# Raw queries, a late scaling on GpSimd, and six places for the inputs

## The chip, the cores and the metric

The kernel runs on one core of one Trainium2 chip. The time is device microseconds of one execution. TensorE does the matrix products, VectorE (DVE), ScalarE (ACT) and GpSimd (POOL) the elementwise work, and SyncE (SP) issues the transfers between HBM and SBUF, the on-chip memory. Matmul results land in PSUM, the banks of which VectorE and ScalarE read here.

## The reference

Retention (linear attention with a decay per head) over a sequence of 768 steps, 2 batches, 8 heads of 64, followed by two feed-forward layers on 1536 tokens of 512 features, 2048 hidden:

```
state = gamma * state + k[t] (outer) v[t]
y[t]  = (1/8) * q[t] . state
x = y as [1536, 512]
h = x @ w_in;   x = silu(h) @ w_out
h = x @ w2_in;  x = leaky_relu(h, 0.01) @ w2_out
```

All arrays are float32.

## The kernel before

**Attention stage.** The sequence is cut into chunks of 128 steps: 12 chunks in all, taken in an order that alternates between the two batches (`ORDER`); j counts them from 0 to 11. The inputs of a chunk come as two transfers of 512 KB (queries with keys, values with keys by row) into one of four places (`att_t`, `load_att`, L98 to L104). For each chunk TensorE computes scores (L200, one chunk ahead), the product of masked scores with values (L219), the product of queries with the running state (L228, not in the first chunk of a batch) and the update of the state (L237, not in the last chunk of a batch). VectorE multiplies the scores with the mask (tile `P`, L207) and adds the update to the decayed state (L250). GpSimd multiplies the keys with their decays (L182) and decays the state (L189).

A row of the result also needs a factor that decays with its position in the chunk, the tile `G`. `G` is spread over the partitions by two small matmuls in chunk 0 (L397) and copied by ScalarE (L401). From chunk 5 on GpSimd multiplies the queries with `G` ahead of the scores (`queries`, L176). For chunks 0 to 4 VectorE multiplies the result with `G` (L258) into an SBUF tile.

The feed-forward products work with float32 numbers cut into a rounded high part and the rest: ScalarE copies the result of a chunk with rounding into `xh` (L262), VectorE subtracts that from the result into `xl` (L263). For chunks 5 to 11 both read the result in PSUM, for chunks 0 to 4 the SBUF tile.

**Feed-forward stage.** Tokens stand in three sets of 512 (chunks 0 to 3, 4 to 7, 8 to 11). `up` (L276) is 12 matmuls per set and block of 128 hidden features, `down` (L304) 12 more. Sets 0 and 1 go through `up` together for one block, then one `down` of set 0: 36 matmuls per turn, and each turn needs two new weights. ScalarE activates each `up` result twice (L287 to L290, into `gf` and into the high part), VectorE subtracts (L291).

Weights come as 64-bit floats and are turned into two float32 parts: two ScalarE copies (`words`, L130, L131), four VectorE steps (`conv1`, L136 and L140; `conv2`, L148 and L152), a ScalarE copy (L161) and a VectorE subtraction (L162, `split_w`). The first two weights are converted in pieces beside the chunks (`piece`), the third in the last chunk, and from there a weight is converted five steps ahead of its use.

**What sets the order.** Nothing is rearranged: each engine executes its instructions in the order in which the code issues them, and waits with semaphores for what an instruction needs. The loop over j (L390 to L421) is that order for the attention stage, the loop over `ops` (L427 to L463) for the rest. A transfer also waits for the eighth before it, by the semaphores of the program.

Of the kernel before, what the change touches and what calls it, by code (L numbers as in the profile page):

```python
# [9 lines left out]
F32 = mybir.dt.float32  # L10
FR = mybir.dt.float32r
# [20 lines left out]
LATE = 5  # L32
# [12 lines left out]
def retention_moe_kernel(ctx: ExitStack, tc: tile.TileContext, att, w1, w2, cst, out):  # L45
# [38 lines left out]
    raw = [gs.tile([128, 2, 512], F32, tag=f"r{i}", name="att_t") for i in range(8)]  # L84
    free = [gs.tile([128, 2, 512], FR, name=f"s{i}") for i in range(21)]

    def widen():
        free.extend(gs.tile([128, 2, 512], FR, tag=f"r{i}", name=f"sr{i}") for i in range(8))
# [9 lines left out]
    def att_t(j, i):  # L98

        return raw[j % 4 * 2 + i // 2][:, i % 2]  # L100

    def load_att(j, *halves):
        for i in halves:
            nc.sync.dma_start(out=raw[j % 4 * 2 + i], in_=att[ORDER[j], :, 2 * i:2 * i + 2])  # L104
# [60 lines left out]
    pt, yu = {}, {}  # L165
# [6 lines left out]

    def queries(j):

        if j >= LATE:
            nc.gpsimd.tensor_tensor(out=att_t(j, 0), in0=att_t(j, 0), in1=G, op=ALU.mult)  # L176
# [33 lines left out]
    def values(j):  # L210
# [3 lines left out]
        yu[j] = y, u = [bank(j % 2 * 2 + i) for i in range(2)]  # L214
# [37 lines left out]
    def store_x(j):  # L252
        b, c = divmod(j, CS)
        y = yu[j][0].rearrange("p (a i) -> p a i", a=NP)
        h, l = (x[b][:, :, c * C:c * C + C] for x in (xh, xl))
        if j < LATE:
            yg = gp.tile([128, NP, C], F32, tag="gf", name="yg")
            nc.vector.tensor_tensor(  # L258
                out=yg, in0=y, in1=G.rearrange("p (a i) -> p a i", a=NP), op=ALU.mult
            )  # L260
            y = yg
        nc.scalar.activation(out=h, in_=y, func=AF.Copy)  # L262
        nc.vector.tensor_tensor(out=l, in0=y, in1=h.bitcast(F32), op=ALU.subtract)  # L263
# [86 lines left out]
    with tc.manual_schedule():  # L350
# [24 lines left out]
        load_att(3, 1)  # L375
        for h in range(H):
            m = M[:, h % 2, (h // 2) * C:(h // 2) * C + C]
            if h < H // 2:
                nc.vector.tensor_scalar(
                    out=m, in0=mask, scalar1=MD[:, h:h + 1], scalar2=None, op0=ALU.mult  # L380
                )
            else:
                nc.scalar.activation(out=m, in_=mask, func=AF.Copy, scale=MD[:, h:h + 1])
# [4 lines left out]
        piece = {5: (conv1, 0), 6: (conv2, 0), 7: (split_w, 0),  # L388
                 8: (conv1, 1), 9: (conv2, 1), 10: (split_w, 1)}
        for j in range(NJ):  # L390
            if j + 1 < NJ:
                queries(j + 1)
                scores(j + 1)
            if j == 0:
                gb = bank(2)
                for r in range(2):
                    nc.tensor.matmul(  # L397
                        out=gb[64 * r:64 * r + 64, :], lhsT=one, rhs=g2[:, r, :],
                        start=True, stop=True,
                    )  # L400
                nc.scalar.activation(out=G, in_=gb, func=AF.Copy)  # L401
            keys(j)
            decay(j)
            values(j)
            if j + 4 < NJ:
                load_att(j + 4, 0, 1)
            if j in (1, 3, 5, 7, 10):
                load_w(early[(1, 3, 5, 7, 10).index(j)])
            if j in (8, 11):
                keep_w(early[(8, 11).index(j)])  # L410
            if j in (5, 8, 10, 11):
                words(early[(5, 8, 10, 11).index(j)])
# [4 lines left out]
            store_x(j)  # L417
            state(j)
            if 5 <= j < NJ - 1:
                step, n = piece[j]  # L420
                step(early[n])  # L421
        split_w(early[2])
        load_w(early[5])
        keep_w(early[2])
        widen()

        for i, op in enumerate(ops):  # L427
# [33 lines left out]
            if i == 1:  # L461
                split_w(early[3])
                keep_w(early[3])  # L463
        for m in range(4):
# [50 lines left out]
```

## Time and profile before

| | us |
|---|---|
| median of three runs | 578.56 (578.34 to 579.38) |
| the profiled execution | 579.3, its span 577.5 |
| TensorE busy | 570.0 (99%) |
| VectorE busy | 285.5 (49%) |
| ScalarE busy | 236.3 (41%) |
| GpSimd busy | 25.3 (4%) |

The attention stage ends at 50.69 us with the first feed-forward matmul (L276). GpSimd's work lies in that stage alone. The granted clock of TensorE is 1.00 over the whole span, its upper level of 2.4 GHz. The shares above are averages over both stages; the rows further down show the stages apart. Times of a row are microseconds from the start of the span.

### The profile page before, as it was taken

Reading aid. Unit: us, or ns where it says so; the run is one execution under the profiler, and the core shown is the slowest. Engines: PE = TensorE matmul, PEld = TensorE weight load, DVE = VectorE, ACT = ScalarE, POOL = GpSimd, SP = SyncE. Lnnn points to the kernel's source line nnn. Section 1 sums busy time; section 2 is a strip of 40 time slices with the busy share of each in tenths; the row PEclk is TensorE's granted clock in tenths of the full one; section 3 lists DMA queues with packets and bytes.
Section 4 is the critical chain, followed back from the end, with each engine's and each line's share of the span. In section 5 each row is a group of like instructions: output and inputs, shape, how many; then the busy total and the mean of one; then the engine's idle time right before and its main releaser. Section 6 shows DMA issues by size and latency. Waiting matters only on the chain.

```text
span 577.5 us, 8037 instructions
## 1 busy us (share of the span) xinstructions
PE 570.0 (99%) x3030; PEld 470.8 (82%) x3030; DVE 285.5 (49%) x474; ACT 236.3 (41%) x427; POOL 25.3 (4%) x30
## 2 busy tenths in 40 slices
PE   8999999999999999999999999999999999999997
PEld 6778888888788888888888888888888888888885
DVE  5788888888884110145866627766660101100000
ACT  2226576667654221245654525555542211212001
POOL 2670000000000000000000000000000000000000
PEclk9999999999999999999999999999999999999999
DMA  8995777777759766726798796698867966562901
GB/s 322 364 346 200 273 244 264 245 254 243 268 178 335 261 193 205 257 92 236 250 374 288 253 325 233 245 321 309 280 218 272 370 194 189 197 196 91 384 2 73
DMA packets 39931, 142.17 MB, mean 246 GB/s; under 512 B 4434, under 2 KB 4562, under 8 KB 39892
## 3 DMA queue, kind: packets, MB, share of 16 engines
q1 hardware_dynamic: 39600, 141.31, 69.1%
q8 instruction: 24, 0.39, 0.3%
q10 hardware_dynamic: 292, 0.34, 0.2%
q14 instruction: 15, 0.12, 0.1%
HBM read 104.94 MB, written 36.70 MB: 245 GB/s over the span
## 4 chain that ended last, share of the span: by engine, by line
PE 94%; DMA 3%; DVE 1%; POOL 1%; ACT 0%; issue 0%; SPq 0%; DVEq 0%; POOLq 0%; ACTq 0%
PE b L276 45%; PE p L304 23%; PE b L304 23%; DMA att_t<-att_dram 3%; PE b L219 1%; PE b L228 1%; PE p L200 1%; POOL att_t L176 1%; DVE P L207 0%; ACT xh L262 0%; DVE xl L263 0%; PE b L397 0%; DVE yg L258 0%; DVE r L152 0%; DVE r L148 0%
## 5 line engine op out<-in xcount | busy, mean ns | idle before, releaser
L276 PE MATMUL b<-xh,s 128*128 128x512 f32 x560 | 181.9, 390 | 0.0
L276 PEld LDWEIGHTS b<-xh,s 128*128 128x128 f32 x560 | 105.1, 188 | 22.5 <-ACT s L288 0.3
L291 DVE TENSOR_TENSOR s<-gf,s 128x512 fp32r<-128x512 f32 x73 | 50.4, 691 | 141.4 <-ACT s L290 94.4
L276 PE MATMUL b<-xl,s 128*128 128x512 f32 x280 | 108.9, 389 | 0.0
L304 PE MATMUL b<-s,s 128*128 128x512 f32 x288 | 73.1, 389 | 0.0
L304 PE MATMUL p<-s,s 128*128 128x512 f32 x288 | 73.1, 389 | 0.0
L290 ACT ACTIVATE gf<-b 128x512 f32<-128x512 f32 x48 | 28.6, 596 | 102.6 <-PE b L276 102.6
L276 PE MATMUL b<-xh,sr 128*128 128x512 f32 x208 | 68.0, 390 | 0.0
L304 PEld LDWEIGHTS b<-s,s 128*128 128x128 f32 x288 | 54.1, 188 | 11.2
L304 PEld LDWEIGHTS p<-s,s 128*128 128x128 f32 x288 | 54.0, 188 | 11.2
L276 PEld LDWEIGHTS b<-xl,s 128*128 128x128 f32 x280 | 52.5, 188 | 10.8
L288 ACT ACTIVATE gf<-b 128x512 f32<-128x512 f32 x48 | 28.2, 588 | 60.1 <-PE b L276 60.1
L161 ACT ACTIVATE s<-r 128x512 fp32r<-128x512 f32 x46 | 29.1, 632 | 55.3 <-DVE r L152 55.2
L152 DVE CUSTOM_DVE_ANT_0 r<-r,u 128x1024 uint16<-128x1024 uint16 x64 | 44.3, 693 | 6.8
L276 PEld LDWEIGHTS b<-xh,sr 128*128 128x128 f32 x208 | 39.0, 188 | 8.4 <-ACT s L288 0.3
L148 DVE SCALAR_TENSOR_TENSOR r<-ws,r 128x512 int32<-128x512 int32 x64 | 44.4, 693 | 2.1
L130 ACT ACTIVATE r<-ws 128x512 f32<-128x512 f32 x64 | 43.0, 672 | 2.8 <-DMA ws<-w_dram 1.9
L131 ACT ACTIVATE u<-ws 128x512 int32<-128x512 uint32 x64 | 43.2, 675 | 0.0
L276 PE MATMUL b<-xl,sr 128*128 128x512 f32 x104 | 40.5, 389 | 0.0
L162 DVE TENSOR_TENSOR s<-r,s 128x512 fp32r<-128x512 f32 x46 | 31.8, 691 | 15.0 <-ACT s L161 13.3
L291 DVE TENSOR_TENSOR sr<-gf,sr 128x512 fp32r<-128x512 f32 x23 | 15.9, 691 | 40.6 <-ACT sr L290 21.1
L304 PE MATMUL b<-sr,s 128*128 128x512 f32 x120 | 30.4, 389 | 0.0
(61 smaller groups left out, 560.6 us busy)
## 6 DMA issues: line engine op xcount, KB each, us to landing
s<-scr SPq DMA_DIRECT2D x71, 512.0 KB, 4.4
ws<-w_dram SPq DMA_DIRECT2D x64, 512.0 KB, 4.8
scr<-s SPq DMA_DIRECT2D x46, 512.0 KB, 3.3
sr<-scr SPq DMA_DIRECT2D x41, 512.0 KB, 4.6
att_t<-att_dram SPq DMA_DIRECT2D x24, 512.0 KB, 7.6
scr<-sr SPq DMA_DIRECT2D x18, 512.0 KB, 3.1
out_dram<-ob SPq DMA_DIRECT2D x11, 256.0 KB, 2.1
out_dram<-ob ACTq DMA_DIRECT2D x1, 256.0 KB, 2.0
```

Source lines behind the costliest of these rows:

```text
L130: nc.scalar.activation(out=r.bitcast(F32), in_=t[:, :, 1].bitcast(F32), func=AF.Abs)
L131: nc.scalar.activation(out=u, in_=t[:, :, 0].bitcast(U32), func=AF.Copy, scale=2.0 ** -29)
L148: nc.vector.scalar_tensor_tensor(out=r, in0=t[:, :, 1], scalar=-0x40000000, in1=r, op0=ALU.bitwise_and, op1=ALU.bitwise_or)
L152: nc.vector.tensor_tensor(out=r, in0=r, in1=u, op=ALU.add)
L161: nc.scalar.activation(out=t[:, 0], in_=r, func=AF.Copy)
L162: nc.vector.tensor_tensor(out=t[:, 1], in0=r, in1=t[:, 0].bitcast(F32), op=ALU.subtract)
L176: nc.gpsimd.tensor_tensor(out=att_t(j, 0), in0=att_t(j, 0), in1=G, op=ALU.mult)
L276: nc.tensor.matmul(out=h, lhsT=w[:, tw, k * 128:k * 128 + 128], rhs=(xh, xl)[tx][b][:, k, :], start=(n == 0), stop=(n == 3 * NP - 1),)
L288: nc.scalar.activation(out=t, in_=h, func=AF.Silu)
L290: nc.scalar.activation(out=t, in_=h, func=AF.Prelu, alpha=0.01)
L291: return lambda: nc.vector.tensor_tensor(out=g[:, 1, :], in0=gf, in1=g[:, 0, :].bitcast(F32), op=ALU.subtract)
L304: nc.tensor.matmul(out=ys[m], lhsT=l, rhs=r, start=(f == 0 and n == 0), stop=(f == NF - 1 and n == 2),)
```

## The change

Queries stay as they are. ScalarE copies each chunk's result from PSUM into an SBUF tile (`evict`), GpSimd multiplies that tile with `G` (`scale`) three chunks later, and four chunks later ScalarE rounds it into `xh` and VectorE subtracts into `xl` (`put`), now from SBUF for all chunks. The last chunks' steps are drawn together: chunks 7 to 9 are scaled in chunk 10 and put in chunk 11, chunks 10 and 11 are put in the feed-forward loop at i = 2 and 3. The inputs have six places (`RING`), so that twelve transfers stand at the head of SP's queue; the places are handed to the feed-forward stage as before, and four tiles for the results besides. The matmuls that spread `G` stand in chunk 3 now, ahead of the scores of chunk 4. The pieces of the first two weights come one chunk earlier. The lines of the changed kernel are numbered differently: L196 is the scores, L203 the mask product, L216, L225 and L234 the products, L178 and L185 the keys and the state's decay, L254 `evict`, L258 `scale`, L264 and L265 `put`, L398 the spreading of `G`, L137 to L163 the conversion of weights, L278 `up`, L293 the subtraction behind an activation.

```diff
@@ -29,7 +29,8 @@
 CS = T // C
 ORDER = [b * NC + c for c in range(NC) for b in range(B)]
 WARM = 18
-LATE = 5
+RING = 6
+BEHIND = 3
 LAG = 2
 SPLIT = 5
 FETCH = 5
@@ -81,11 +82,11 @@
-    raw = [gs.tile([128, 2, 512], F32, tag=f"r{i}", name="att_t") for i in range(8)]
-    free = [gs.tile([128, 2, 512], FR, name=f"s{i}") for i in range(21)]
-
-    def widen():
-        free.extend(gs.tile([128, 2, 512], FR, tag=f"r{i}", name=f"sr{i}") for i in range(8))
+    raw = [gs.tile([128, 2, 512], F32, tag=f"r{i}", name="att_t") for i in range(2 * RING)]
+    free = [gs.tile([128, 2, 512], FR, name=f"s{i}") for i in range(25 - 2 * RING)]
+
+    def widen(tag, n):
+        free.extend(gs.tile([128, 2, 512], FR, tag=f"{tag}{i}", name=f"s{tag}{i}") for i in range(n))
     def pair(i):
@@ -97,11 +98,11 @@
     def att_t(j, i):
-        return raw[j % 4 * 2 + i // 2][:, i % 2]
+        return raw[j % RING * 2 + i // 2][:, i % 2]
     def load_att(j, *halves):
         for i in halves:
-            nc.sync.dma_start(out=raw[j % 4 * 2 + i], in_=att[ORDER[j], :, 2 * i:2 * i + 2])
+            nc.sync.dma_start(out=raw[j % RING * 2 + i], in_=att[ORDER[j], :, 2 * i:2 * i + 2])
     stage, W, scr = {}, {}, {}
@@ -162,18 +163,13 @@
         nc.vector.tensor_tensor(out=t[:, 1], in0=r, in1=t[:, 0].bitcast(F32), op=ALU.subtract)
-    pt, yu = {}, {}
+    pt, yu, two = {}, {}, []
     def first(j):
         return ORDER[j] % NC == 0
     def last(j):
         return ORDER[j] % NC == NC - 1
-
-    def queries(j):
-
-        if j >= LATE:
-            nc.gpsimd.tensor_tensor(out=att_t(j, 0), in0=att_t(j, 0), in1=G, op=ALU.mult)
     def keys(j):
@@ -211,7 +207,8 @@
         q, v, kn = (att_t(j, i) for i in (0, 2, 3))
         s0 = st[ORDER[j] // NC][0]
         P = pt.pop(j)
-        yu[j] = y, u = [bank(j % 2 * 2 + i) for i in range(2)]
+        y, u = (bank(j % 2 * 2 + i) for i in range(2))
+        yu[j] = [y, u, None]
         for p in range(NP):
             c = slice(p * C, p * C + C)
             for r in range(2):
@@ -249,16 +246,21 @@
         else:
             nc.vector.tensor_tensor(out=s0, in0=s1, in1=u, op=ALU.add)
-    def store_x(j):
+    def evict(j):
+
+        if j % 2 == 0:
+            two.append(gs.tile([128, 2, 512], F32, tag=f"y{j // 2 % 4}", name="yg"))
+        yg = yu[j][2] = two[-1][:, j % 2]
+        nc.scalar.activation(out=yg, in_=yu[j][0], func=AF.Copy)
+
+    def scale(j):
+        yg = yu[j][2]
+        nc.gpsimd.tensor_tensor(out=yg, in0=yg, in1=G, op=ALU.mult)
+
+    def put(j):
         b, c = divmod(j, CS)
-        y = yu[j][0].rearrange("p (a i) -> p a i", a=NP)
         h, l = (x[b][:, :, c * C:c * C + C] for x in (xh, xl))
-        if j < LATE:
-            yg = gp.tile([128, NP, C], F32, tag="gf", name="yg")
-            nc.vector.tensor_tensor(
-                out=yg, in0=y, in1=G.rearrange("p (a i) -> p a i", a=NP), op=ALU.mult
-            )
-            y = yg
+        y = yu[j][2].rearrange("p (a i) -> p a i", a=NP)
         nc.scalar.activation(out=h, in_=y, func=AF.Copy)
         nc.vector.tensor_tensor(out=l, in0=y, in1=h.bitcast(F32), op=ALU.subtract)
@@ -373,6 +375,8 @@
         load_att(3, 0)
         load_att(2, 1)
         load_att(3, 1)
+        for j in range(4, RING):
+            load_att(j, 0, 1)
         for h in range(H):
             m = M[:, h % 2, (h // 2) * C:(h // 2) * C + C]
             if h < H // 2:
@@ -385,44 +389,51 @@
         scores(0)
         masked(0, 2)
-        piece = {5: (conv1, 0), 6: (conv2, 0), 7: (split_w, 0),
-                 8: (conv1, 1), 9: (conv2, 1), 10: (split_w, 1)}
+        piece = {4: (conv1, 0), 5: (conv2, 0), 6: (split_w, 0),
+                 7: (conv1, 1), 8: (conv2, 1), 9: (split_w, 1)}
         for j in range(NJ):
-            if j + 1 < NJ:
-                queries(j + 1)
-                scores(j + 1)
-            if j == 0:
-                gb = bank(2)
+            if j == BEHIND:
+                gb = bank(3)
                 for r in range(2):
                     nc.tensor.matmul(
                         out=gb[64 * r:64 * r + 64, :], lhsT=one, rhs=g2[:, r, :],
                         start=True, stop=True,
                     )
                 nc.scalar.activation(out=G, in_=gb, func=AF.Copy)
+            if j + 1 < NJ:
+                scores(j + 1)
             keys(j)
             decay(j)
+
+            for i in {NJ - 2: (j - 3, j - 2, j - 1), NJ - 1: (j - 1,)}.get(j, (j - BEHIND,)):
+                if i >= 0:
+                    scale(i)
             values(j)
-            if j + 4 < NJ:
-                load_att(j + 4, 0, 1)
-            if j in (1, 3, 5, 7, 10):
-                load_w(early[(1, 3, 5, 7, 10).index(j)])
+            if j in (0, 2, 6, 7, 10):
+                load_w(early[(0, 2, 6, 7, 10).index(j)])
+            if j + RING < NJ:
+                load_att(j + RING, 0, 1)
             if j in (8, 11):
                 keep_w(early[(8, 11).index(j)])
-            if j in (5, 8, 10, 11):
-                words(early[(5, 8, 10, 11).index(j)])
+            if j in (4, 7, 10, 11):
+                words(early[(4, 7, 10, 11).index(j)])
             if j + 1 < NJ:
                 masked(j + 1)
             if j == NJ - 1:
                 conv(early[2])
-            store_x(j)
+            evict(j)
+            for i in {NJ - 1: (j - 4, j - 3, j - 2)}.get(j, (j - BEHIND - 1,)):
+                if i >= 0:
+                    put(i)
             state(j)
-            if 5 <= j < NJ - 1:
+            if j in piece:
                 step, n = piece[j]
                 step(early[n])
+        scale(NJ - 1)
         split_w(early[2])
         load_w(early[5])
         keep_w(early[2])
-        widen()
+        widen("r", 2 * RING)
         for i, op in enumerate(ops):
             l, p, b, f = op
@@ -461,6 +472,10 @@
             if i == 1:
                 split_w(early[3])
                 keep_w(early[3])
+            if i in (2, 3):
+                put(NJ + i - 4)
+            if i == 3:
+                widen("y", 4)
         for m in range(4):
             for l, p, b, f in ops[-LAST:]:
                 down(m, l, b, f)
```

GpSimd's instructions for the last three chunks that have work there, in the kernel before (`att_t` tiles with `G` are queries, with `cs` keys; `st` the state):

```order
L176 TENSOR_TENSOR att_t_96<-att_t_96,G_82 128x512
L182 TENSOR_TENSOR att_t_95<-att_t_95,cs_81 128x512
L189 TENSOR_TENSOR st01_85<-st00_84,cs_81 128x256
L176 TENSOR_TENSOR att_t_98<-att_t_98,G_82 128x512
L182 TENSOR_TENSOR att_t_97<-att_t_97,cs_81 128x512
L189 TENSOR_TENSOR st11_87<-st10_86,cs_81 128x256
L176 TENSOR_TENSOR att_t_100<-att_t_100,G_82 128x512
```

The same end of GpSimd's program in the changed kernel (`yg` tiles are results, two chunks to a tile):

```order
L178 TENSOR_TENSOR att_t_99<-att_t_99,cs_81 128x512
L185 TENSOR_TENSOR st01_85<-st00_84,cs_81 128x256
L258 TENSOR_TENSOR yg_393<-yg_393,G_82 128x512
L178 TENSOR_TENSOR att_t_101<-att_t_101,cs_81 128x512
L185 TENSOR_TENSOR st11_87<-st10_86,cs_81 128x256
L258 TENSOR_TENSOR yg_490<-yg_490,G_82 128x512 x2
L258 TENSOR_TENSOR yg_591<-yg_591,G_82 128x512 x2
L258 TENSOR_TENSOR yg_682<-yg_682,G_82 128x512 x2
```

The multiplication of queries is gone from between the keys, and six multiplications of results stand behind the last state decay.

VectorE's instructions around the conversion of the third weight (`r_678`), from the mask product of chunk 11 to the split of that weight (`s2`), in the kernel before:

```order
L207 TENSOR_TENSOR P_682<-p1_649,M_83 128x1024
L263 TENSOR_TENSOR xl2_93<-b0_658,xh2_90 128x4x128
L162 TENSOR_TENSOR s1_103<-r_592,s1_103 128x512
L136 TENSOR_SCALAR r_678<-r_678 128x512
L140 TENSOR_SCALAR r_678<-r_678 128x512
L148 SCALAR_TENSOR_TENSOR r_678<-ws_443,r_678 128x512
L152 ISA r_678<-r_678,u_679 128x1024
L263 TENSOR_TENSOR xl2_93<-b2_688,xh2_90 128x4x128
L162 TENSOR_TENSOR s2_104<-r_678,s2_104 128x512
```

The same place in the changed kernel, where the third weight is `r_676` and its split writes `s2_108`:

```order
L163 TENSOR_TENSOR s1_107<-r_537,s1_107 128x512
L203 TENSOR_TENSOR P_680<-p1_644,M_83 128x1024
L265 TENSOR_TENSOR xl1_92<-yg_490,xh1_89 128x4x128
L137 TENSOR_SCALAR r_676<-r_676 128x512
L141 TENSOR_SCALAR r_676<-r_676 128x512
L149 SCALAR_TENSOR_TENSOR r_676<-ws_486,r_676 128x512
L153 ISA r_676<-r_676,u_677 128x1024
L265 TENSOR_TENSOR xl1_92<-yg_490,xh1_89 128x4x128
L265 TENSOR_TENSOR xl2_93<-yg_591,xh2_90 128x4x128 x2
L163 TENSOR_TENSOR s2_108<-r_676,s2_108 128x512
```

The subtraction of chunk 10 ahead of the conversion is now that of chunk 6; the one of chunk 11 behind it is now three, of chunks 7, 8 and 9; they read `yg` in SBUF instead of a bank (`b`) of PSUM. The split of the second weight (`s1`) has moved ahead of the mask product.

VectorE's instructions some steps later in the changed kernel, around the fifth and sixth converted weights (`r_776`, `r_807`) in the feed-forward loop:

```order
L153 ISA r_776<-r_776,u_777 128x1024
L293 TENSOR_TENSOR s5_111<-gf_804,s5_111 128x512
L163 TENSOR_TENSOR s6_112<-r_776,s6_112 128x512
L265 TENSOR_TENSOR xl2_93<-yg_682,xh2_90 128x4x128
L137 TENSOR_SCALAR r_807<-r_807 128x512
L141 TENSOR_SCALAR r_807<-r_807 128x512
L149 SCALAR_TENSOR_TENSOR r_807<-ws_725,r_807 128x512
L153 ISA r_807<-r_807,u_808 128x1024
L293 TENSOR_TENSOR s7_113<-gf_835,s7_113 128x512
L163 TENSOR_TENSOR s8_114<-r_807,s8_114 128x512
L265 TENSOR_TENSOR xl2_93<-yg_682,xh2_90 128x4x128
```

The same steps in the kernel before, where these weights are `r_767` and `r_798`:

```order
L152 ISA r_767<-r_767,u_768 128x1024
L291 TENSOR_TENSOR s5_107<-gf_795,s5_107 128x512
L162 TENSOR_TENSOR s6_108<-r_767,s6_108 128x512
L136 TENSOR_SCALAR r_798<-r_798 128x512
L140 TENSOR_SCALAR r_798<-r_798 128x512
L148 SCALAR_TENSOR_TENSOR r_798<-ws_720,r_798 128x512
L152 ISA r_798<-r_798,u_799 128x1024
L291 TENSOR_TENSOR s7_109<-gf_824,s7_109 128x512
L162 TENSOR_TENSOR s8_110<-r_798,s8_110 128x512
```

The subtractions of chunks 10 and 11 have come in behind the two splits.

## Rows read from the trace of the kernel before

**Rows 1.** Chain that ended last: start, us, what; feed-forward stage, 120 to 170 us.

```profile
129.86 5.44 PE b L276 x24
...
138.02 5.45 PE b L276 x24
...
146.20 5.59 PE b L276 x24
...
162.88 5.64 PE b L276 x24
```

**Rows 2.** Timeline of VectorE: start, us, engine line op out<-in xcount [idle before <-releaser].

```profile
11.16 1.18 DVE L263 TENSOR_TENSOR xl<-yg,xh 128x512 fp32r<-128x512 f32 x1 [0.70 <-ACT xh L262]
...
19.25 0.69 DVE L263 TENSOR_TENSOR xl<-yg,xh 128x512 fp32r<-128x512 f32 x1 [0.70 <-ACT xh L262]
...
27.14 0.41 DVE L250 TENSOR_TENSOR st<-st,b 128x256 f32<-128x256 f32 x1
...
41.40 1.05 DVE L136 TENSOR_SCALAR r<-r 128x512 f32<-128x512 f32 x1
...
50.06 0.42 DVE L136 TENSOR_SCALAR r<-r 128x512 f32<-128x512 f32 x1
50.52 0.43 DVE L140 TENSOR_SCALAR r<-r 128x512 int32<-128x512 int32 x1
...
51.71 0.69 DVE L152 CUSTOM_DVE_ANT_0 r<-r,u 128x1024 uint16<-128x1024 uint16 x1
...
60.39 0.69 DVE L162 TENSOR_TENSOR s<-r,s 128x512 fp32r<-128x512 f32 x1
61.00 0.42 DVE L136 TENSOR_SCALAR r<-r 128x512 f32<-128x512 f32 x1
...
68.75 0.69 DVE L162 TENSOR_TENSOR s<-r,s 128x512 fp32r<-128x512 f32 x1 [0.70 <-ACT s L161]
...
73.36 0.69 DVE L291 TENSOR_TENSOR s<-gf,s 128x512 fp32r<-128x512 f32 x1 [0.28 <-ACT s L288]
...
77.11 0.69 DVE L162 TENSOR_TENSOR s<-r,s 128x512 fp32r<-128x512 f32 x1 [0.70 <-ACT s L161]
```

**Rows 3.** Timeline of TensorE in the attention stage, columns as in rows 2.

```profile
7.56 1.07 PE L397 MATMUL b<-g,one 1*64 1x512 f32 x4
...
17.29 1.16 PE L200 MATMUL p<-att_t 64*128 64x128 f32 x16 [0.69 <-DMA att_t<-att_dram]
...
28.29 0.69 PE L237 MATMUL b<-att_t 128*64 128x64 f32 x16
28.90 1.16 PE L200 MATMUL p<-att_t 64*128 64x128 f32 x16
...
32.65 1.16 PE L200 MATMUL p<-att_t 64*128 64x128 f32 x16
...
41.22 1.16 PE L200 MATMUL p<-att_t 64*128 64x128 f32 x16 [0.81 <-POOL att_t L176]
...
48.64 1.09 PE L219 MATMUL b<-P,att_t 128*64 128x128 f32 x16 [0.46 <-DVE P L207]
...
50.69 0.50 PE L276 MATMUL b<-xh,s 128*128 128x512 f32 x1
```

**Rows 4.** Busy time by window: last columns TensorE's clock, DMA share, GB/s.

```profile
16.00:18.00 2.00, 1.30 (x28) 1.20 (x30) 2.00 (x4) 0.00 (x0) 0.61 (x1) 1.00 1.02 408
```

**Rows 5.** Timeline of ScalarE, columns as in rows 2.

```profile
44.48 0.60 ACT L262 ACTIVATE xh<-b 128x512 fp32r<-128x512 f32 x1 [4.04 <-PE b L228]
```

**Rows 6.** Timeline of GpSimd, columns as in rows 2.

```profile
10.75 1.04 POOL L182 TENSOR_TENSOR att_t<-att_t,cs 128x512 f32<-128x512 f32 x1 [1.41 <-DMA att_t<-att_dram]
...
14.33 0.61 POOL L189 TENSOR_TENSOR st<-st,cs 128x256 f32<-128x256 f32 x1
...
26.63 1.72 POOL L176 TENSOR_TENSOR att_t<-att_t,G 128x512 f32<-128x512 f32 x1
...
31.07 1.27 POOL L176 TENSOR_TENSOR att_t<-att_t,G 128x512 f32<-128x512 f32 x1 [1.15 <-DMA att_t<-att_dram]
```

## The prediction

> **What bounds the kernel now.** I read the page first, then the stages by window, the chain of waits, and the timelines of the four engines. TensorE is busy 99% of the span, but that is an average over two stages. In the feed-forward stage it runs back to back: a turn of the chain (24 up matmuls, 12 down) is 8.16 us, from 129.86 to 138.02 [rows 1]. Three later pieces of up matmuls, the first 5.59 and the last 5.64, take longer than 5.44, about 0.55 us too much together [rows 1]. The reason, as I read it, is on VectorE: its loop over two new weights (shift, mask, merge, add, split, in exchange with ScalarE) turns in 8.36 us, 68.75 to 77.11 [rows 2]. It is 0.20 slower than TensorE's turn, eats its lead over some ten turns and is late for three. So the end of the stretch with new weights, and with it the run, is set by VectorE's chain, already in the kernel before: what begins that chain later makes the run longer by as much, and an earlier start of TensorE alone is worth nothing beyond the 0.55.
>
> In the attention stage a chunk takes TensorE 3.75 us when nothing waits (28.90 to 32.65) [rows 3]. The transfers set its beginning: scores of the fourth chunk (counting from 0) start at 17.29 after 0.69 of waiting for input, with the DMA engines full at 408 GB/s [rows 3, 4]. From there to the first feed-forward matmul at 50.69 it takes 33.40. Without any wait: seven chunks of 3.75, one without its state update (3.75 less 0.61, the step from 28.29 to 28.90), and 2.05 for the last (48.64 to 50.69), 31.4 in all [rows 3]. So 2.0 us at most are to be had there: 0.81 behind Pool's scaling of queries, 0.46 behind the mask product, the rest small.
>
> **What the change costs and saves.** *Transfers.* Twelve loads stand ahead of the first weight instead of eight, but the engines are full, so more places only lengthen the queue; I leave the fourth chunk at 17.3. The first weight's load moves one chunk forward, the second waits for the decay matmuls of chunk 3, since its staging place holds their input; the three chunks' loads behind it on that queue wait too. That is about 17.5, still several transfers ahead of their use, so nothing.
>
> *Decays.* The two decay matmuls with ScalarE's copy leave chunk 0 and come ahead of the fourth chunk's scores, where TensorE idles 0.69 [rows 3]; they take 1.07 at 7.56 [rows 3], so 0.2 to 0.4 are visible. What leaves chunk 0 is worth nothing, since the transfers set the pace up to 17.29.
>
> *TensorE's wait on Pool goes.* Scores read raw queries, so the 0.81 and its smaller fellows go. ScalarE gets a second copy per chunk (0.60 like the one at 44.48, ahead of which it idled 4.04 [rows 5]); that is hidden, but it puts the low part's subtraction 1.1 us behind the chunk's last matmul instead of 0.6. VectorE loses five products with the decays (0.69 each), in chunks whose start the transfers set: nothing.
>
> *The port.* Here is the main cost. A subtraction that reads a copy in SBUF takes 0.69 when Pool rests (19.25), but 1.18 at 11.16, while Pool's key product runs 10.75 to 11.79; taken as 0.69 of work it began at 11.65, 0.14 before Pool's end. At 41.40 the first step of a weight takes 1.05 instead of 0.42, and Pool in turn 1.72 instead of 1.27 at 26.63. A state update that reads PSUM takes its 0.41 at 27.14 in the middle of that Pool operation [rows 2, 6]. So operations of the two engines on SBUF operands alone exclude each other, and those from PSUM are free. The Trainium skill says the same in "SBUF — State Buffer", section "SBUF: two separate sides": the shared port pair is an exclusive lock, held for a whole instruction, against VectorE instructions with two SBUF inputs. The trace agrees (1.18 against 0.69); by that rule the change comes out slower, without it nearly even, as worked out below.
>
> The change moves all subtractions to SBUF copies (before: five of twelve) and gives Pool twelve scalings where it had seven. From 18.2 (the decays ready) to the end of the third weight's conversion the port must carry, on Pool, 12 scalings of 1.27, 6 key products of 1.04 and 6 state decays of 0.61, 25.1; on VectorE 7 subtractions of 0.69, two weights at 2.92 (0.42, 0.43, three of 0.69) and the third's 2.23, 12.9: 38.0 [rows 2, 6]. With 0.14 saved at each of 45 hand-overs it is 31.7. In the kernel before that stretch ends at 52.40 [rows 2], 34.2 after 18.2, and by the same count (7 scalings, 2 such subtractions) carried 23.3 to 28.2. So the port has no free time left, and the scalings held back to the end meet the conversions there.
>
> *The last chunks step by step*, with these durations and one operation on the port at a time. Scores of chunk 10 start near 40.3 instead of 41.22, a gain of 0.9. Then the second weight's merge waits for the scaling of chunk 7 and its add for that of chunk 8, 0.75 and 0.97; the mask product of chunk 10, queued behind them on VectorE, ends at 46.4 where TensorE wanted it at 45.2; that of chunk 11 at 49.1, 0.6 too late; the first feed-forward matmul starts at 51.2, +0.5. The subtraction for chunk 6 follows the eviction of chunk 10 (48.6) and waits for the scaling of chunk 10, so the third weight's conversion begins at 51.0 instead of 50.06: **+0.9**. Its last step waits for the scaling of chunk 11: **+1.0**. Before, one subtraction (chunk 11) stood between this conversion and the loop; now five do (chunks 7 to 11), at 0.61 from start to start (60.39 to 61.00): 4 x 0.61 = **+2.4**. Against that VectorE waits for ScalarE, 0.28 in a turn like that at 73.36, so **-0.3** [rows 2]. Sum +4.0, and I add 0.1 for ScalarE's two late rounding copies, which push its activations: **+4.1**. The second feed-forward group waits about 0.9 for chunk 7's subtraction; that lies within the sum, as does the 0.5.
>
> The sum is made against the profiled execution, 579.3 (span 577.5 and 1.8 around it): 583.4. That execution stands 0.7 above the median 578.56, so I forecast **582.7**.
>
> **Rivals.**
> - *The waits on the port do not pile up.* Pool's operations would fit under the mask product and state update, 1.6 us per chunk that need no port. For: in the kernel before most subtractions show no wait. Against: those read PSUM, and the count is 31.7 to 38.0. Attention then ends at 48.7, the conversion starts near 48.7 too, -1.3; +2.4 -0.3 and the 0.1 stay: +0.9, 579.5.
> - *Faster.* Attention as in the case above, and the late subtractions fall into VectorE's idle time, 0.70 and 0.28 per turn (68.75, 73.36) [rows 2]. The chain then starts 1.3 earlier and nothing is added: 577.3. Against: the first of them stand between conversion and split, where VectorE does not wait, and their rounding copies stand ahead of an activation.
> - *Slower still: Pool falls so far behind that keys are late.* Key products queue behind scalings on Pool, and TensorE's state update waits for them; this decides once Pool has lost its lead of some 4 to 6 us. At the upper count the third conversion ends at 18.2 + 38.0 = 56.2 instead of 54.2: +2.0 more, 584.7. Against: the hand-over of 0.14 is seen in each collision I read.
> - *The change doesn't do what it says* only in part: six places can't bring input sooner while the engines are full. That costs nothing and is in the sum.
>
> **How the numbers follow.** Forecast 0.71, its own range 581.2 to 584.0 (the port's waits may be half, and the loop may take up one more of the subtractions); waits that don't pile up 0.11; faster 0.09; Pool too late 0.09. For 8 in 10 I leave out the faster case and most of the last: 579.4 to 584.2. A measurement of this kernel tells about 0.2%, 1.2 us: faster is the third case and a little, 0.10; the case of 579.5 is mostly "same", 0.09; the rest slower, 0.81.
>
> **What would show it.** Right: subtractions of about 1.0 to 1.7 on VectorE beside Pool's operations; Pool nearly without idle time between 18 and 46; the fourth chunk's scores again near 17.3; the third weight's conversion starting near 51 and its last step stretched by a scaling; the second group of up matmuls late by about a microsecond; pieces of about 5.65 from the start of the feed-forward stage, not only around 150. Wrong: subtractions of 0.69 throughout, a conversion that starts at 48.7, or pieces of 5.44 with the subtractions in place, which would mean that the loop has idle time that I don't see.

## The result: 583.37 us

The changed kernel takes 583.37 us (583.31 to 583.48, 4 runs), the kernel before on the same chip 578.47: ratio 1.0084, 95% interval 1.0072 to 1.0096. It is slower by 4.9 us; forecast was 582.7, and the time lies in the range.

The profiled execution took 583.31 us, span 581.5. VectorE is busy for 286.6 us, ScalarE for 242.5, GpSimd for 34.4 (6%). Where the time went is read from the chain that ended last, as in [rows 1] (start, us, what), first of the kernel after:

```profile
66.50 5.69 PE b L278 x24
...
166.87 5.65 PE b L278 x24
...
175.25 5.44 PE b L278 x24
```

then the row of before that answers to the last of these:

```profile
171.24 5.44 PE b L276 x24
```

The pieces of 24 up matmuls take about 5.65 us from the start of the feed-forward stage, thirteen of them, where three did before. The row of 5.44 us is the first undisturbed one, behind the last weight that is new. It starts 4.01 us later than before (175.25 - 171.24), and from there on the two executions take the same time: 583.31 - 175.25 = 408.06 and 579.30 - 171.24 = 408.06. All of the loss lies ahead of that row.

TensorE in the attention stage (timeline of after: start, us, engine line op out<-in xcount, idle before and its releaser), as in [rows 3]:

```profile
16.32 1.07 PE L398 MATMUL b<-g,one 1*64 1x512 f32 x4
17.32 1.16 PE L196 MATMUL p<-att_t 64*128 64x128 f32 x16
...
40.25 1.16 PE L196 MATMUL p<-att_t 64*128 64x128 f32 x16
...
46.31 1.09 PE L216 MATMUL b<-P,att_t 128*64 128x128 f32 x16 [1.15 <-ACT s L162]
...
48.98 1.09 PE L216 MATMUL b<-P,att_t 128*64 128x128 f32 x16 [0.55 <-issue]
...
51.02 0.50 PE L278 MATMUL b<-xh,s 128*128 128x512 f32 x1
...
55.05 0.50 PE L278 MATMUL b<-xl,s 128*128 128x512 f32 x1 [0.77 <-DVE xl L265]
```

The wait on GpSimd ahead of the scores of chunk 10 is gone (40.25 instead of 41.22), and the decay matmuls hide in the wait for the fourth chunk's input. But the mask products of the last two chunks are late by 1.15 and 0.55 us, and the first up group starts at 51.02 instead of 50.69. The releaser named for the first of these waits is the one that came last by the profile; the instruction that was late is VectorE's, in its timeline, as in [rows 2]:

```profile
41.96 1.43 DVE L149 SCALAR_TENSOR_TENSOR r<-ws,r 128x512 int32<-128x512 int32 x1
43.43 1.65 DVE L153 CUSTOM_DVE_ANT_0 r<-r,u 128x1024 uint16<-128x1024 uint16 x1
45.00 1.21 DVE L203 TENSOR_TENSOR P<-p,M 128x1024 f32<-128x1024 f32 x1
...
49.68 1.36 DVE L265 TENSOR_TENSOR xl<-yg,xh 128x512 fp32r<-128x512 f32 x1 [0.80 <-ACT xh L264]
50.96 0.41 DVE L137 TENSOR_SCALAR r<-r 128x512 f32<-128x512 f32 x1
...
51.88 1.80 DVE L149 SCALAR_TENSOR_TENSOR r<-ws,r 128x512 int32<-128x512 int32 x1
53.70 0.69 DVE L153 CUSTOM_DVE_ANT_0 r<-r,u 128x1024 uint16<-128x1024 uint16 x1
54.32 1.89 DVE L265 TENSOR_TENSOR xl<-yg,xh 128x512 fp32r<-128x512 f32 x3
56.12 0.68 DVE L163 TENSOR_TENSOR s<-r,s 128x512 fp32r<-128x512 f32 x1
```

and GpSimd's beside it, as in [rows 6]:

```profile
38.90 0.79 POOL L185 TENSOR_TENSOR st<-st,cs 128x256 f32<-128x256 f32 x1
39.66 6.56 POOL L258 TENSOR_TENSOR yg<-yg,G 128x512 f32<-128x512 f32 x4
49.21 1.28 POOL L258 TENSOR_TENSOR yg<-yg,G 128x512 f32<-128x512 f32 x1 [2.99 <-ACT yg L254]
51.82 1.30 POOL L258 TENSOR_TENSOR yg<-yg,G 128x512 f32<-128x512 f32 x1 [1.33 <-ACT yg L254]
```

From 39.66 to 46.22 GpSimd does four scalings, 1.64 us each in the mean instead of 1.27, and beside them VectorE's merge (L149) and add (L153) of the second weight take 1.43 and 1.65 instead of 0.69. Taken apart, the four scalings start at 39.66, 41.07, 42.81 and 44.49 and take 1.45, 1.77, 1.72 and 1.73, so that the operations of the two engines end by turns: GpSimd at 42.84, VectorE at 43.39, GpSimd at 44.53, VectorE at 45.08, GpSimd at 46.22. The mask product (L203, from PSUM) takes its 1.21 as ever, but it is queued behind the two, so it ends at 46.21, and TensorE goes on at 46.31. At 49.68 a subtraction waits for the scaling of chunk 10, at 51.88 the third weight's merge for that of chunk 11, and at 54.32 stand three subtractions where before there was one. The third weight's split comes at 56.12, before at 53.10:

```profile
53.10 0.69 DVE L162 TENSOR_TENSOR s<-r,s 128x512 fp32r<-128x512 f32 x1
```

That is 3.02 of the 4.01 us; the rest, 0.99, comes behind it, where two more subtractions stand in the next rounds of the loop (64.01, 68.26).

Transfers (window of after: length, busy us and instructions of PE, PEld, DVE, ACT, POOL, then granted clock, DMA share, GB/s) answer [rows 4]:

```profile
16.00:18.00 2.00, 2.00 (x30) 1.12 (x28) 0.42 (x1) 0.98 (x2) 0.48 (x1) 1.00 1.01 404
...
40.00:44.00 4.00, 4.00 (x77) 3.40 (x72) 3.96 (x5) 1.43 (x4) 4.00 (x3) 1.00 0.22 84
```

Ahead of the fourth chunk the DMA engines are as full as before. Between 40 and 44 us they have little left to do (84 GB/s), where before still moved 334:

```profile
40.00:44.00 4.00, 3.19 (x58) 2.75 (x56) 3.50 (x5) 0.44 (x1) 4.00 (x4) 1.00 0.91 334
```

### The profile page after: what moved, and what is told of

Same layout as the page of the kernel before. It is cut to its first block, busy times and chain, and to the rows that moved or that the text cites. A ratio compares the mean times of both kernels' runs of the same rounds, so it can differ in the third digit from the quotient of the medians.

```text
span 581.5 us, 8040 instructions
## 1 busy us (share of the span) xinstructions
PE 572.5 (98%) x3030; PEld 469.8 (81%) x3030; DVE 286.6 (49%) x469; ACT 242.5 (42%) x439; POOL 34.4 (6%) x35
## 4 chain that ended last, share of the span: by engine, by line
PE 94%; DVE 3%; DMA 1%; ACT 1%; issue 1%; SPq 0%; ACTq 0%
PE b L278 44%; PE p L306 22%; PE b L306 22%; PE b L216 2%; PE p L196 1%; PE b L225 1%; DMA att_t<-att_dram 1%; PE b L234 1%; DVE r L149 1%; DVE xl L265 1%; DVE r L153 1%; DVE r L141 0%; DVE r L137 0%; ACT xh L264 0%; DVE P L203 0%
## 5 line engine op out<-in xcount | busy, mean ns | idle before, releaser
L278 PE MATMUL b<-xh,sr 128*128 128x512 f32 x360 | 118.2, 391 | 0.0
L278 PE MATMUL b<-xh,s 128*128 128x512 f32 x312 | 102.5, 393 | 0.2 <-ACT s L290 0.2
L278 PEld LDWEIGHTS b<-xh,sr 128*128 128x128 f32 x360 | 67.5, 188 | 15.7 <-ACT sy L290 0.9
L278 PEld LDWEIGHTS b<-xh,s 128*128 128x128 f32 x312 | 58.5, 188 | 14.8 <-ACT s L290 1.6
L293 DVE TENSOR_TENSOR s<-gf,s 128x512 fp32r<-128x512 f32 x42 | 29.0, 691 | 84.2 <-ACT s L292 57.1
L278 PE MATMUL b<-xl,sr 128*128 128x512 f32 x180 | 70.1, 389 | 0.0
L278 PE MATMUL b<-xl,s 128*128 128x512 f32 x156 | 60.9, 390 | 0.8 <-DVE xl L265 0.8
L293 DVE TENSOR_TENSOR sr<-gf,sr 128x512 fp32r<-128x512 f32 x38 | 26.3, 691 | 71.0 <-ACT sr L292 39.2
L153 DVE CUSTOM_DVE_ANT_0 r<-r,u 128x1024 uint16<-128x1024 uint16 x64 | 45.6, 712 | 6.8
L149 DVE SCALAR_TENSOR_TENSOR r<-ws,r 128x512 int32<-128x512 int32 x64 | 46.2, 721 | 2.1
L306 PE MATMUL b<-s,s 128*128 128x512 f32 x168 | 42.8, 389 | 0.0
L306 PE MATMUL p<-s,s 128*128 128x512 f32 x168 | 42.8, 389 | 0.0
L278 PEld LDWEIGHTS b<-xl,sr 128*128 128x128 f32 x180 | 33.8, 188 | 6.9
L278 PEld LDWEIGHTS b<-xl,s 128*128 128x128 f32 x156 | 29.3, 188 | 7.0 <-DVE xl L265 1.2
L278 PE MATMUL b<-xh,sy 128*128 128x512 f32 x96 | 31.6, 391 | 0.0
```

The lines of the kernel that those rows point to most:

```text
L149: nc.vector.scalar_tensor_tensor(out=r, in0=t[:, :, 1], scalar=-0x40000000, in1=r, op0=ALU.bitwise_and, op1=ALU.bitwise_or)
L153: nc.vector.tensor_tensor(out=r, in0=r, in1=u, op=ALU.add)
L278: nc.tensor.matmul(out=h, lhsT=w[:, tw, k * 128:k * 128 + 128], rhs=(xh, xl)[tx][b][:, k, :], start=(n == 0), stop=(n == 3 * NP - 1),)
L293: return lambda: nc.vector.tensor_tensor(out=g[:, 1, :], in0=gf, in1=g[:, 0, :].bitcast(F32), op=ALU.subtract)
L306: nc.tensor.matmul(out=ys[m], lhsT=l, rhs=r, start=(f == 0 and n == 0), stop=(f == NF - 1 and n == 2),)
```

## The experiments

Theory: two things cost, the port that VectorE and GpSimd share (about 3.2 us, the difference between the forecast and the case in which its waits don't pile up) and the subtractions of chunks 8 to 11 in VectorE's loop (2.4). Main rival: only one of the two does. The first four runs take away one, the other or both, or add one; the others look for what the kernel before still has to give.

**Subtractions late.** Rounding copies and subtractions of chunks 8 to 11 move to steps 44 and 45 of the feed-forward stage, behind the new weights.

```diff
-            for i in {NJ - 1: (j - 4, j - 3, j - 2)}.get(j, (j - BEHIND - 1,)):
+            for i in {NJ - 1: (j - 4,)}.get(j, (j - BEHIND - 1,)):
...
-            if i in (2, 3):
-                put(NJ + i - 4)
-            if i == 3:
+            if i in (44, 45):
+                put(2 * i - 80)
+                put(2 * i - 79)
+            if i == 45:
```

> The changed kernel, but the rounding copies and subtractions of chunks 8 to 11 stand at steps 44 and 45 of the feed-forward loop, after the last conversion of a new weight and ahead of the first up of the third set. Theory (VectorE's chain of weight conversions sets the end, and the port delays that chain): four subtractions of 0.61 leave the chain, 0.28 of which VectorE had to wait anyway: 583.4 - 2.2 = 581.2; the pieces of up matmuls still run at about 5.63, the third conversion still starts near 51.0. Rival 1 (only the port costs time; the subtractions fall into VectorE's idle time): no change, 583.4. Rival 2 (the start of the first up matmul sets the end, 51.0 against 50.7): no change, 583.4.

Measured: 581.11 us, ratio to before 1.0047 (1.0034 to 1.0061), 2.3 less than the changed kernel. Its chain:

```profile
114.84 5.44 PE b L278 x24
...
123.00 5.48 PE b L278 x24
...
164.63 5.62 PE b L278 x24
172.97 5.44 PE b L278 x24
```

The conversion of the third weight still begins beside the scalings:

```profile
50.85 0.41 DVE L137 TENSOR_SCALAR r<-r 128x512 f32<-128x512 f32 x1
```

But TensorE's lead lasts until 123, where pieces of 5.63 were expected throughout; the row of 172.97 stands 2.28 before that of after. So four subtractions, with their rounding copies on ScalarE, cost 2.3.

**No scaling** (the multiplication by `G` is left out).

```diff
     def scale(j):
         yg = yu[j][2]
-        nc.gpsimd.tensor_tensor(out=yg, in0=yg, in1=G, op=ALU.mult)
+        pass
```

> The changed kernel without GpSimd's twelve multiplications of results by G: the factor of position is left out of the computation, all else stands. Theory: without them the port has time, the waits in the second and third conversions go, TensorE reaches the feed-forward stage near 49.2 and the third conversion starts near 48.7 instead of 51.0, its end moves by 3.2 in all: 580.2. The five subtractions stay, so it stays slower than before (578.5). Rival 1 (only the port): the attention stage's 2.0 are won and nothing lost, about 576.9. Rival 2 (the start of the first up matmul sets the end): 51.0 to 49.2, 581.6.

Measured: 580.10 us, ratio 1.0028 (1.0017 to 1.004), 3.3 less than the changed kernel. VectorE's timeline:

```profile
41.52 0.68 DVE L149 SCALAR_TENSOR_TENSOR r<-ws,r 128x512 int32<-128x512 int32 x1
42.24 0.69 DVE L153 CUSTOM_DVE_ANT_0 r<-r,u 128x1024 uint16<-128x1024 uint16 x1
...
48.08 0.69 DVE L265 TENSOR_TENSOR xl<-yg,xh 128x512 fp32r<-128x512 f32 x1 [1.05 <-ACT xh L264]
48.69 0.42 DVE L137 TENSOR_SCALAR r<-r 128x512 f32<-128x512 f32 x1
49.14 0.43 DVE L141 TENSOR_SCALAR r<-r 128x512 int32<-128x512 int32 x1
49.60 0.69 DVE L149 SCALAR_TENSOR_TENSOR r<-ws,r 128x512 int32<-128x512 int32 x1
50.33 0.69 DVE L153 CUSTOM_DVE_ANT_0 r<-r,u 128x1024 uint16<-128x1024 uint16 x1
50.94 1.89 DVE L265 TENSOR_TENSOR xl<-yg,xh 128x512 fp32r<-128x512 f32 x3
```

VectorE's instructions are those of the changed kernel and in the same order; with GpSimd's scalings gone the merge and the add take their 0.69, and the conversion begins at 48.69. The three subtractions in a row are still there, and so is the loss against before. The Trainium skill has a rule for this in "SBUF — State Buffer", section "SBUF: two separate sides": a VectorE operation with two inputs in SBUF and a GpSimd operation that reads SBUF lock each other out for a whole instruction. These rows agree (1.43, 1.65 and 1.80 with the scalings, 0.68 to 0.69 without).

**Both** edits together (the multiplication by `G` left out here too).

> Both edits together: no multiplications by G (left out of the computation), and the subtractions of chunks 8 to 11 after the last conversion. Theory: both terms are gone, the chain starts 1.3 earlier than before and carries no more than before: 577.2 to 578.0, a little below the kernel before. Rival 1: as the run without multiplications, about 576.9. Rival 2: 581.6.

Measured: 577.91 us, ratio 0.999 (0.9981 to 0.9999). The two terms add up: 583.37 - 577.91 = 5.46 against 3.27 + 2.26 = 5.53 from the two runs before. The six places, the raw queries and a GpSimd without any scaling together gain no more here than the 0.6 us by which this run lies below before (578.50 beside it).

**The subtractions alone, on the kernel before**: four further VectorE operations of the same size, at the places where the changed kernel has its late ones.

```diff
+    def again(j):
+        l = xl[2][:, :, (j - 8) * C:(j - 7) * C]
+        lf = l.bitcast(F32)
+        nc.vector.tensor_tensor(out=l, in0=lf, in1=lf, op=ALU.max)
...
+                again(8)
+                again(9)
...
+            if i in (2, 3):
+                again(NJ + i - 4)
```

> The kernel before with four more VectorE operations of the subtraction's shape (128x512, SBUF to SBUF, each rewrites a part of xl with its own values) where the change puts its extra subtractions: two behind the third conversion, one each at steps 2 and 3. GpSimd does nothing at that time. Theory: the chain carries 4 x 0.61 more, less 0.28 of waiting: 578.5 + 2.1 = 580.6, with pieces of up matmuls above 5.6 from much earlier than 146. Rivals 1 and 2: 578.5, no change.

Measured: 580.31 us, ratio 1.0034 (1.0022 to 1.0047): +1.8 on a kernel that has nothing else of the change. Of their 2.44 us (4 x 0.61) VectorE's loop had idle time for 0.6 only. TensorE's scores of chunk 10 did not wait for GpSimd in this execution, the first up group began at 50.12 and the third conversion at 49.18:

```profile
40.34 1.16 PE L200 MATMUL p<-att_t 64*128 64x128 f32 x16
...
50.12 0.50 PE L281 MATMUL b<-xh,s 128*128 128x512 f32 x1
```

```profile
49.18 0.42 DVE L136 TENSOR_SCALAR r<-r 128x512 f32<-128x512 f32 x1
```

**The kernel before, profiled again**, since the wait of 0.81 us in [rows 3] had not shown itself there.

> The kernel before, unchanged, profiled once more. What it tells apart: the profiled execution of before on which the prediction stood took 579.3 us, 0.8 above the median of 16 runs; its scores of chunk 10 began at 41.22 us and its first up group at 50.69. Theory: that execution lost some 0.6 us in the attention stage on late transfers. Then another execution has scores of chunk 10 near 40.3 to 40.6, the first up group near 50.1, the conversion of the third weight at 49.4 to 49.6, and a time near 578.5. Rival: the attention stage always looks so, and 579.3 is scatter of the feed-forward stage; then 41.2, 50.7 and 50.06 come back.

Measured: 578.99 us, beside a median of 578.34 over 27 runs of the same kernel (577.45 to 580.21). TensorE and GpSimd:

```profile
40.89 1.16 PE L200 MATMUL p<-att_t 64*128 64x128 f32 x16 [0.69 <-POOL att_t L176]
```

```profile
39.56 1.27 POOL L176 TENSOR_TENSOR att_t<-att_t,G 128x512 f32<-128x512 f32 x1 [1.68 <-DMA att_t<-att_dram]
```

Neither theory nor rival: this execution lies above the median too and has the wait too, behind a scaling that waited for its transfer. The first up group begins 0.34 earlier than in [rows 3], the third conversion 0.33 (49.73), and the time is 0.31 less. That executions near the median are without the wait is likely from this and from the run with four subtractions, but no execution of this kernel near its median was profiled.

**Six places alone**, on the kernel before: `RING = 6`, weight loads and pieces of the first two weights one chunk earlier, as the change has them; queries scaled as before.

```diff
-        return raw[j % 4 * 2 + i // 2][:, i % 2]
+        return raw[j % RING * 2 + i // 2][:, i % 2]
...
-        piece = {5: (conv1, 0), 6: (conv2, 0), 7: (split_w, 0),
-                 8: (conv1, 1), 9: (conv2, 1), 10: (split_w, 1)}
+        piece = {4: (conv1, 0), 5: (conv2, 0), 6: (split_w, 0),
+                 7: (conv1, 1), 8: (conv2, 1), 9: (split_w, 1)}
```

> The kernel before with the six places for inputs, and with the weight loads and the pieces of work for the first two weights one chunk earlier, as the change has them; nothing else of the change. Queries are scaled by Pool ahead of the scores and VectorE subtracts in PSUM, as before. Theory: the places do help what comes early (inputs are in place some 3 us earlier, so TensorE and Pool wait for no transfer in chunks 4 to 9), but only as far as VectorE's chain of work for the third and fourth weight follows: third conversion 0.5 to 1.0 us earlier than in before, 577.6 to 578.2 us, while the late pieces of the feed-forward stage stay at 5.6. Rival 1: the places are worth nothing, 578.5. Rival 2: part of the 4.9 us that the change lost came with the earlier pieces of work, 579 or more.

Measured: 578.98 us, ratio 1.0007 (0.9998 to 1.0015). The expected gain is not there; the rival of 579 or more is nearly met. TensorE and VectorE say why:

```profile
30.87 1.09 PE L220 MATMUL b<-P,att_t 128*64 128x128 f32 x16 [0.93 <-DVE P L208]
...
35.14 1.09 PE L220 MATMUL b<-P,att_t 128*64 128x128 f32 x16 [0.45 <-DVE P L208]
```

```profile
27.35 1.16 DVE L137 TENSOR_SCALAR r<-r 128x512 f32<-128x512 f32 x1
28.54 1.15 DVE L141 TENSOR_SCALAR r<-r 128x512 int32<-128x512 int32 x1
29.61 1.21 DVE L208 TENSOR_TENSOR P<-p,M 128x1024 f32<-128x1024 f32 x1
```

The inputs come early and no scores wait for GpSimd any more, but GpSimd, without a pause from 24.94 to 41.53, now meets VectorE's pieces, which stand one chunk earlier: 1.16 and 1.15 us instead of 0.42 and 0.43, and the mask product behind them is late. The wait on transfers turned into a wait on the port.

**Late subtractions on the kernel before**: ScalarE copies the results of chunks 8 to 11 to SBUF (`evict`), rounding and subtraction follow at steps 44 and 45.

```diff
-            store_x(j)
+            (store_x if j < 8 else evict)(j)
...
+            if i in (44, 45):
+                store_x(2 * i - 80)
+                store_x(2 * i - 79)
```

> The kernel before, in which ScalarE copies the results of chunks 8 to 11 to SBUF (already scaled, since the queries are) and the rounding copies and subtractions of these four chunks follow at steps 44 and 45 of the feed-forward stage. Nothing of the change's scaling or places. Theory: VectorE's chain gets 2.4 us shorter, but in before it is only some 0.55 us (three late pieces of 5.6 instead of 5.44) behind TensorE, so the time falls by 0.3 to 0.6 only: 577.9 to 578.2, with pieces of 5.44 from the beginning. Rival: all of the 2.4 us comes back, 576.1.

Measured: 579.44 us, ratio 1.0015 (1.0006 to 1.0024), a miss. VectorE does not use the room; it waits for ScalarE's rounding copies of the weights instead:

```profile
48.74 0.69 DVE L162 TENSOR_TENSOR s<-r,s 128x512 fp32r<-128x512 f32 x1 [1.22 <-ACT s L161]
49.34 0.42 DVE L136 TENSOR_SCALAR r<-r 128x512 f32<-128x512 f32 x1
...
52.38 0.69 DVE L162 TENSOR_TENSOR s<-r,s 128x512 fp32r<-128x512 f32 x1 [0.70 <-ACT s L161]
```

and at the other end of the run the chain has a new wait, TensorE behind an output's write-out:

```profile
527.54 0.61 ACT ob L324
528.15 0.02 issue
528.16 2.95 DMA out_dram<-ob
...
531.87 0.96 PE p L310 x3
```

The first costs the gain (the conversion begins at 49.34), the second some 0.6 us more: from the first undisturbed piece (170.50) this execution of 579.14 has 408.64 left, not 408.06. In before ScalarE waits for a write-out at this place too, but for 0.83 us instead of 1.72, and TensorE does not wait for ScalarE there. Why the write-out lands later here is open.

**Six places and late subtractions** together:

> Both edits of the two runs before this one together: queries scaled by Pool ahead of the scores, six places for inputs, the pieces of work for the first two weights one chunk earlier, and the rounding copies and subtractions of chunks 8 to 11 late. Theory: with VectorE's chain out of the way, what TensorE gains by earlier inputs counts in full: first up group 1 to 2 us earlier than in before, pieces of 5.44 throughout, 576.0 to 577.3, which beats both kernels. Rival: TensorE's chunks are set by the mask products and the values, not by inputs, and the first up group begins where it does in before: 577.9 to 578.2.

Measured: 579.28 us, ratio 1.0008 (0.9999 to 1.0018), outside both expectations. The mishaps of both come together: the mask product is late by 0.93 and 0.45 again; the third conversion begins at 47.91, but the splits at 51.69 and 56.23 wait 1.35 and 0.94 for ScalarE's rounding copies; and 408.63 us (579.44 - 170.81) lie behind the last late piece.

**Six places, pieces unmoved**: as in six places alone, with the pieces in chunks 5 to 10.

> The kernel before with six places for inputs, and the pieces of work for the first two weights in chunks 5 to 10 as before (in the run with six places alone they stood in chunks 4 to 9, and TensorE waited 0.93 and 0.45 us for the mask products behind them, since the two tensor_scalars of chunk 4 took 1.16 and 1.15 us beside Pool instead of 0.42 and 0.43). Theory: without the collision those 1.4 us are gone and the waits on inputs stay gone (before: 0.69 to 0.8 in chunk 9's turn); the first up group begins at 49.2 to 49.8 and the third conversion 0.4 to 0.9 us earlier than 50.06, so that 577.5 to 578.1 is measured. Rival: the collision only moves to another chunk, because Pool's scalings are earlier too; first up at 50.4 and 578.6 to 579.0, as with six places alone.

Measured: 578.27 us, ratio 0.9998 (0.9989 to 1.0007). The two waits of six places alone are gone, the first up group begins at 49.53, as expected, and the conversion at 48.91, earlier than expected, yet the time is that of before's median, outside both expectations. VectorE's timeline has collisions still (1.37 for a 0.43, 1.42 for a 0.69), now where they delay the mask products by less:

```profile
30.15 1.37 DVE L141 TENSOR_SCALAR r<-r 128x512 int32<-128x512 int32 x1
...
34.80 1.42 DVE L153 CUSTOM_DVE_ANT_0 r<-r,u 128x1024 uint16<-128x1024 uint16 x1
```

Against the profiled execution of [rows 2] the conversion is 1.15 earlier and the time 1.05 less: the one-to-one of the prediction again. Its 11 runs lie within 0.72 us (578.04 to 578.76), the 15 of before beside them within 1.62 (577.8 to 579.42). The expectation had counted from that late execution, as the prediction did (see *The sum* below). The smaller spread suggests that with two more places the run depends less on when a transfer comes; that is not shown. None of these versions beats the kernel before.

## Why the prediction was right

*The bound.* That VectorE's chain for the new weights sets the end is shown by all profiled executions in two distances. Behind the start of the first undisturbed piece lie 408.04 to 408.10 us in nine of the eleven, whatever lies ahead; the two others are those with the write-out. And from the start of the third conversion on VectorE to that piece it takes 121.16 to 121.33 us in six, however late the conversion starts (in late subtractions on before, a wait of 0.70 for ScalarE stands in the place of one subtraction):

| execution | its time | third conversion | first undisturbed piece | between |
|---|---|---|---|---|
| before | 579.30 | 50.06 | 171.24 | 121.18 |
| before again | 578.99 | 49.73 | 170.95 | 121.22 |
| six places alone | 579.19 | 49.80 | 171.13 | 121.33 |
| pieces unmoved | 578.25 | 48.91 | 170.17 | 121.26 |
| late subtractions on before | 579.14 | 49.34 | 170.50 | 121.16 |
| both | 577.93 | 48.60 | 169.86 | 121.26 |
| subtractions late | 581.02 | 50.85 | 172.97 | 122.12 |
| no scaling | 580.16 | 48.69 | 172.09 | 123.40 |
| four subtractions on before | 580.31 | 49.18 | 172.21 | 123.03 |
| after | 583.31 | 50.96 | 175.25 | 124.29 |
| six places, late subtractions | 579.44 | 47.91 | 170.81 | 122.90 |

What is put on the chain lengthens the second distance: the merge's wait for a scaling by 0.9 (subtractions late), the four subtractions by 2.2 (no scaling), both by 3.1 (after), the two waits for ScalarE by 1.7 (last row). The start of the first up group does not set the end: it is 49.17 in no scaling and 49.08 in both, and the first undisturbed pieces of these two are 2.23 apart (172.09 - 169.86).

*Transfers and decays.* The fourth chunk's scores started at 17.32 (17.3 forecast). Of the decays' 0.2 to 0.4 nothing is seen apart from the wait for input. That six places bring no input sooner held for this chunk alone; the later inputs came early (84 GB/s left to move between 40 and 44 us, 334 before).

*The port.* The term was worth 3.3 us (583.37 - 580.10), the forecast 3.2. Its steps stand in the rows: mask products ending at 46.21 and 48.88 (46.4 and 49.1), first up group at 51.02 (51.2), conversion at 50.96 (51.0). One detail was off: the step of the third weight that waits for the last scaling is the merge (1.80 instead of 0.69, +1.1), not the add: that scaling began at 51.82, just ahead of the merge.

*The subtractions.* +2.4 was forecast, 2.2 with the 0.3 of waiting and the 0.1 for rounding copies; 2.3 is shown by taking them out of the changed kernel with their rounding copies, 1.8 by adding them to before without. What the copies cost by themselves no run shows.

*The sum.* +4.1 was forecast against the profiled execution, 4.0 measured (583.31 - 579.30): 0.9 in the start of the third conversion and 3.1 behind it. The step that was mis-sized is the last one: 0.7 was taken off because that execution stood above the median of before. Four executions of after lie within 0.17 us of each other and have no such surplus, so against the median the change costs 4.9, and the forecast came out 0.7 low. The likely place of the surplus is the start of that conversion: 50.06 in this execution, 49.73 in the second one, but 49.18 in the run with four subtractions, which is the kernel before up to there and whose profiled execution took the median time of its run. An estimate from 49.18 and the two distances, 121.2 and 408.06, is 578.4, the median of before; against such an execution the change moves the start by 1.8, not 0.9. In the two late executions TensorE waited for GpSimd's scaling of queries (0.81 and 0.69 us, the second behind a late transfer), a wait that the change does away with and that the median execution need not have. No execution of before near the median was profiled, so this is argued, not shown.

*The rivals.* "Waits don't pile up" is what the run without scaling shows (conversion at 48.69, forecast for that case 48.7; 580.10, forecast 579.5, low by the same last step), so it fails by the scalings alone. "Faster" needed idle time in VectorE's loop; four extra operations on before cost 1.8 of their 2.44 us. "Keys late" did not come: TensorE's state updates show no wait in its timeline, though GpSimd had no pause from 31.06 to 46.22.

## What to carry to other kernels

Before moving work between VectorE and GpSimd, count what both do on SBUF operands alone in the stretch concerned, as if it were one engine; where the sum reaches the stretch's length, an operation added there delays the other engine, and whatever is queued behind the loser: here the twelve scalings came out as 3.3 us. Find the chain that sets the end, and see whether the new work stands on it: four operations of 0.6 us on a half idle engine (49% busy) cost 1.8 to 2.3. Take a second profile before trusting a wait of less than a microsecond that the change removes: the profiled execution may not be the median one.

## What the runs showed of the hardware

Neither engine had precedence on the port where both had work waiting: in the four scalings from 39.66 GpSimd took 1.45 to 1.77 us each for 1.27, while VectorE's two steps beside them took 1.43 and 1.65 for 0.69, in turns. And single executions of one program scattered by more than some edits are worth: 577.45 to 580.21 over 27 runs of before, 583.31 to 583.48 over 4 of after; that inputs which come just in time are the reason is argued, not shown.
